# One written order of pieces for the set-up and the first two batches of a packed-attention and gated-MLP kernel, with its conversion adds on one engine

## Chip, core and metric

The kernel runs on one core of a Trainium2 chip. The engines that matter are TensorE (PE in the profile, with its weight loads as PEld), VectorE (DVE), ScalarE (ACT), GpSimd (POOL) and SyncE (SP), whose queue issues every data transfer. The metric is the device time of one execution in microseconds, median of several runs, lower is better.

## What is computed

Eight batches, 576 positions, 8 heads of 64 channels, 512 model channels. Attention goes through 32 packed queries per head; a gated product with a five-tap convolution and a second MLP with a mix over positions follow. Shortened from the reference:

```python
def sm_attn(qq, kk, vv):
    s = scale * np.matmul(qq, kk.transpose(0, 1, 3, 2))
    a = np.exp(s - np.max(s, axis=-1, keepdims=True))
    a = a / (np.sum(a, axis=-1, keepdims=True) + 1e-09)
    return np.matmul(a, vv)
p_packed = sm_attn(p, k, v)              # 32 packed rows per head
x = sm_attn(q, p_packed, p_packed)       # back to 576 positions
...
gate = 1.0 / (1.0 + np.exp(-gate_pre))   # gate_pre: conv_w over 5 taps of x
x = gate * (x @ w_val) @ w_out
...
h = np.maximum(x @ w_in, 0.0)
u, v = h[..., :512], h[..., 512:]
v_n = (v - mu) / np.sqrt(var + 1e-06)    # normalised over channels
v_s = np.einsum('ts,bsd->btd', w_spatial, v_n) + b_spatial[None, :, None]
out = (u * v_s) @ w_out2
```

## The kernel before

**Set-up.** The weight matrices arrive as 64-bit floats. Each of four matrices (`w_outT`, the two halves of `w_in`, `w_val`) is loaded in four pieces of 128 rows, 128x1024 words or 512 KB each (`load_raw`, L484), and each piece is converted to 32 bits by `from_f64` (L456): one ACT instruction (L460), then three on DVE (L464, L467, L468), then an add (L471). The add runs on POOL, or on DVE for the five pieces that `DADD` names: two of `w_outT` (`o0`, `o1`), two of the second half of `w_in` (`w0`, `w1`) and one of its first half (`u2`). The four converted pieces are called `woT`, `winv` (second half of `w_in`), `wval` and `winu` (first half). Pieces of `winu` share one temporary buffer (`cv_p`, one buffer), so the next piece's ACT instruction waits for the add of the piece before. `fold` (L499) multiplies `woT` with `winv` or `winu` on PE into the split weight `wp`, which takes the place of both matrices from then on: four folds for the `v` half (`fv`), four for the `u` half (`fu`). `spatial` (L509) loads and splits the position mix into `ws`; for its last rows it loads 128 rows (L517) and then 97 rows (L520). `final` (L527) does the same as `from_f64` for `w_out2`.

**Attention of a batch** (`Attn`): `sa` (packed scores and softmax, L141 to L163), `tr` (transposes, L172), `av` (L181), `ppt` (L204), `sb` (scores back, L212, and two softmaxes in `softmax_n`, L224 to L230), `sb2` (L236 to L243, with the split `Ah`/`Al`), `m` (packed rows times `wval`, L256, split into `Mh`/`Ml`), then the gate: for the first batch by `cx` on PE (L291, with the sigmoid at L299), for the others by `xt` and a convolution on DVE (L310).

**MLP of a batch** (`Mlp`): `val` (products of the `M` and `A` splits, 48 matmuls in four groups, one for each 128 channels, then gate and split), `hv` (five row blocks, normalised over channels into `vn`), `hu` (four groups), `sp` (four groups of the mix over positions), `out` (four groups). All PE results go through one pool of four accumulators (`ps2`).

**Order.** Three lists of tokens, `START` (set-up and the first batch's attention), `FIRST` (first batch's MLP, the second's attention) and `LOOP` (each later batch's MLP and the next batch's attention), give the order in which the pieces are written; each token writes out a whole piece. The kernel is built with a scheduler that places the instructions of all engines from there. Matmuls of 32-bit inputs appear twice in the counts of the trace.

Of the kernel before, what the change touches and what calls it, by code (L numbers as in the profile page):

```python
# [31 lines left out]
def packed_attention_gated_mlp(  # L32
# [72 lines left out]
    def load_kq(kind, b, g):  # L105
        src = kT if kind == "k" else qT
        t = kq_p.tile([P, 2, S], F32, tag="kq", name="kq")
        nc.sync.dma_start(out=t, in_=src[b, g])
        kq_t[kind, b, g] = t

    def load_v(b, g):
        t = v_p.tile([P, 4, 5, 65], F32, tag="v", name="v")
        nc.sync.dma_start(out=t, in_=vT[b, g])
        v_t[b, g] = t

    def load_p(b):
        t = sm_p.tile([P, NC * NPK], F32, tag="pbd", name="pbd")
        nc.sync.dma_start(out=t, in_=pT[b])
        pbd_t[b] = t

    class Attn:
        def __init__(self, b):
# [3 lines left out]
            self.gate = {}  # L126

# [8 lines left out]
        def sa(self, _):  # L136
            ps, heads = self.heads(pbd_t.pop(self.b), "k")
            for i in range(0, 8, 2):
                for qt in range(4):
                    for g, h, pT_, k in heads[i:i + 2]:  # L140
# [4 lines left out]
                        )  # L145
            mx = sm_p.tile([P, 8], F32, tag="mx", name="mx")
# [13 lines left out]
            for g in range(2):  # L160
                a = f_p.tile([P, S], F32, tag="f", name="a")
# [8 lines left out]
        def tr(self, g):  # L170
            aT = sm_p.tile([P, NB, NPK], F32, tag="aT", name="aT")
            nc.vector.transpose(out=aT.rearrange("p a b -> p (a b)"), in_=self.a.pop(g))  # L172
            self.aT[g] = aT

        def av(self, g):
# [12 lines left out]
            if g == 0:  # L188
# [3 lines left out]
            nc.vector.reciprocal(rs, rs)  # L192
            nc.scalar.activation(out=self.pp[:, g, :], in_=ps[:, :64], func=AF.Copy, scale=rs)
            if self.b == 0:
                if g == 0:
# [6 lines left out]
        def ppt(self, _):  # L202
            ps = ps2.tile([P, 2, 512], F32, tag="ps2", name="ps2")[:, 0, :P]
            nc.tensor.transpose(ps, self.pp.rearrange("p a b -> p (a b)"), ident)  # L204
            self.ppT = pp_p.tile([P, P], F32, tag="ppT", name="ppT")
            nc.scalar.copy(out=self.ppT, in_=ps)

        def sb(self, _):
# [8 lines left out]
            for g in range(2):  # L217
                self.softmax_n(g, ps[g])

        def softmax_n(self, g, ps):  # L220
# [8 lines left out]
            )  # L229
            nc.scalar.activation(out=sTf, in_=sTf, func=AF.Exp, scale=scale)  # L230
            self.sT[g] = sT

        def sb2(self, g):
# [9 lines left out]
            nc.vector.transpose(out=an, in_=sT.rearrange("p a b -> p (a b)"))  # L243
            hi = am_p.tile([P, S], F32R, tag="Ah", name="Ah")
            lo = am_p.tile([P, S], F32R, tag="Al", name="Al")
            split(hi, lo, an)
            self.A[g] = (hi, lo)
            self.an[g] = an

        def m(self, _):  # L250
            ps = ps2.tile([P, 2, 512], F32, tag="ps2", name="ps2")
            for h in range(4):
                hs = slice(NPK * h, NPK * h + NPK)
                for g in range(2):
# [4 lines left out]
                    )  # L259
            hi = am_p.tile([P, 2, DM], F32R, tag="Mh", name="Mh", bufs=1)  # L260
            lo = am_p.tile([P, 2, DM], F32R, tag="Ml", name="Ml", bufs=1)
            split(hi, lo, ps)
            self.M = (hi, lo)

        def xt(self, n):
# [9 lines left out]
            if n == 0:  # L275
# [3 lines left out]
            if n == 1:  # L279
                for c in range(4):  # L280
                    self.conv(c, self.x[c // 2][:, c % 2, :])

        def cx(self, n):
            ps = [ps2.tile([P, 2, 512], F32, tag="ps2", name="ps2") for _ in range(2)]
            for tap in reversed(range(CONV)):
                sft = CONV - 1 - tap
                lo = sft if n == 0 else 0
                for h in range(4):
                    hs = slice(NPK * h, NPK * h + NPK)
                    for g in range(2):  # L290
# [12 lines left out]
        def conv(self, c, x):  # L303
            gt = ug_p.tile([P, S], F32, tag="ug", name="gate")
            self.gate[c] = gt
            acc = f_p.tile([P, S], F32, tag="f", name="acc")
            nc.scalar.activation(out=acc, in_=x, func=AF.Copy, scale=cw[:, c, CONV - 1:CONV])  # L307
            for tap in range(CONV - 1):
# [4 lines left out]
                )  # L313
            nc.scalar.activation(out=gt, in_=acc, func=AF.Sigmoid)

    class Mlp:
        def __init__(self, at):
# [3 lines left out]
            self.vn = None  # L321

        def val(self, c):
# [3 lines left out]
            for n in range(2):  # L327
# [7 lines left out]
                )  # L335
            t = f_p.tile([P, S], F32, tag="f", name="g1")
            nc.vector.tensor_tensor(  # L337
                out=halves(t), in0=ps[:, :, :SH], in1=halves(at.gate.pop(c)), op=ALU.mult
            )
            g = g_p.tile([P, 2, S], F32R, tag="g", name="g")  # L340
            split(g[:, 0, :], g[:, 1, :], t)
            if not self.g1:
# [4 lines left out]
            self.g1[c] = g  # L347

        def hv(self, tt):
# [11 lines left out]
            vr = vr_p.tile([P, DM], F32, tag="vr", name="vr")  # L361
            if w == P:
                mm3(ps, [((g1[k][:, 0, ts_], g1[k][:, 1, ts_]), (w_hi[k], w_lo[k])) for k in range(NC)])
                nc.scalar.activation(out=vr, in_=ps, func=AF.Relu)  # L364
            else:
                mms(ps, [(self.tail[:, k, :], wk) for k in range(NC) for wk in (w_hi[k], w_lo[k])])
                nc.scalar.copy(out=vr[:w], in_=ps[w:])
                nc.vector.tensor_tensor(out=vr[:w], in0=ps[:w], in1=vr[:w], op=ALU.add)
                nc.scalar.activation(out=vr[:w], in_=vr[:w], func=AF.Relu)
            st = sm_p.tile([P, 6], F32, tag="st", name="st")  # L370
# [4 lines left out]
            nc.vector.tensor_scalar_add(rstd[:w], mv[:w, 1:2], 1e-6)  # L375
            nc.gpsimd.tensor_tensor(out=rstd[:w], in0=rstd[:w], in1=mhalf[:w], op=ALU.pow)  # L376
            nc.vector.tensor_scalar(  # L377
                out=vr[:w], in0=vr[:w], scalar1=mv[:w, 0:1], scalar2=rstd[:w],
                op0=ALU.subtract, op1=ALU.mult,
            )  # L380
            if tt < NT - 1:
                split(vn[0][:, tt, :], vn[1][:, tt, :], vr)
            else:
                split(vn[0][:64, tt, :], vn[0][64:, tt, :], vr[:w])
                nc.scalar.copy(out=vn[1][:64, tt, :], in_=vr[:w])

        def hu(self, c):
            ps = ps2.tile([P, 2, 512], F32, tag="ps2", name="ps2")
            cs = slice(P * c, P * c + P)
            for n in range(2):  # L390
# [10 lines left out]
                )  # L401
            u = ug_p.tile([P, S], F32, tag="ug", name="u")
            nc.scalar.activation(out=halves(u), in_=ps[:, :, :SH], func=AF.Relu)
            self.u[c] = u

        def sp(self, c):
            ps = ps2.tile([P, 2, 512], F32, tag="ps2", name="ps2")
            cs = slice(P * c, P * c + P)
            for n in range(2):
# [12 lines left out]
                )  # L422
            t = f_p.tile([P, S], F32, tag="f", name="g2")
            nc.vector.tensor_tensor(  # L424
                out=halves(t), in0=ps[:, :, :SH], in1=halves(self.u.pop(c)), op=ALU.mult
            )
            g = g_p.tile([P, 2, S], F32R, tag="g", name="g")
            split(g[:, 0, :], g[:, 1, :], t)
            self.g2[c] = g

        def out(self, e):
            ps = ps2.tile([P, 2, 512], F32, tag="ps2", name="ps2")
            cs = slice(P * e, P * e + P)
            for n in range(2):
# [10 lines left out]
                )  # L445
            t = f_p.tile([P, S], F32, tag="f", name="o")
            nc.scalar.copy(out=halves(t), in_=ps[:, :, :SH])  # L447
            nc.sync.dma_start(out=outT[self.b, e], in_=t)
# [7 lines left out]
    def from_f64(dst, raw, n, pool, tag, last=nc.gpsimd):  # L456
# [5 lines left out]
        )  # L462
        ci, ei = c.bitcast(I32), e.bitcast(I32)
# [6 lines left out]
        )  # L470
        last.tensor_tensor(out=dst, in0=dst, in1=c, op=ALU.add)  # L471

    def raw64(slot, srcs):
        n = len(srcs)
        raw = (vn_p if slot == "vn1" else const).tile([P, n, 512, 2], I32, tag=slot, name="raw")
        for i, src in enumerate(srcs):
# [197 lines left out]
```

## Time and profile before

| | us |
|---|---|
| median of 3 runs | 637.4 (636.73 to 638.5) |
| the profiled execution, its own time | 639.22 |
| its span in the trace | 637.4 |

The profile is of one execution; its time is 1.82 us above its span, and the median of the runs lies 1.8 us below the profiled execution's own time. Times in the trace count from the span's start. "Busy" is the time in which an engine has an instruction; "idle before" is the time in which it had none, with the event that ended it. The granted clock is 1.00 at full speed (2.4 GHz) and 0.50 at half (1.2 GHz).

### The profile page before, as it was taken

The page shows a single profiled execution, that of the slowest core. Times are in us where ns is not written, and L with a number is a line of the kernel's source. Part 1 is how long each engine was busy: PE and PEld are TensorE (multiplying, and loading weights), DVE is VectorE, ACT ScalarE, POOL GpSimd, SP SyncE. Part 2 cuts the span into 40 slices and gives each one's busy share as a digit, 9 for nine tenths or more (in the row PEclk, how much of TensorE's full clock was granted, in tenths as well). Part 3 has the DMA queues.
Part 4 walks back from the last instruction along what each step waited for, and adds up shares of the span by engine and source line. Part 5 has one row for each costly group of instructions (what it writes and reads, how often), then busy time and mean ns, then how long its engine had stood idle before and what let it go on. Part 6 is the DMA issues. An engine that isn't in the chain of part 4 may idle for free.

```text
span 637.4 us, 12474 instructions
## 1 busy us (share of the span) xinstructions
PE 596.7 (94%) x5267; PEld 514.7 (81%) x5267; DVE 446.0 (70%) x873; ACT 292.3 (46%) x503; POOL 49.3 (8%) x67
## 2 busy tenths in 40 slices
PE   3687697999999999999999999999999999999997
PEld 2323663898988898899889888989889988989997
DVE  4998355977957696687759685869667875965640
ACT  2522435636463564346543655355533744363422
POOL 1242002200010000100010001000010001000100
PEclk9985797999999999999999999999999999999999
DMA  8960053302322012401222132202240110010001
GB/s 331 408 226 1 1 194 124 127 1 76 114 88 76 20 59 77 159 1 76 80 85 75 53 102 86 75 20 77 64 149 1 75 39 1 2 57 20 1 1 74
DMA packets 16569, 52.48 MB, mean 82 GB/s; under 512 B 1953, under 2 KB 2977, under 8 KB 16514
## 3 DMA queue, kind: packets, MB, share of 16 engines
q1 hardware_dynamic: 16514, 51.70, 22.7%
q8 instruction: 41, 0.67, 0.4%
q14 instruction: 14, 0.11, 0.1%
HBM read 42.25 MB, written 9.44 MB: 81 GB/s over the span
## 4 chain that ended last, share of the span: by engine, by line
PE 80%; DVE 9%; DMA 5%; ACT 3%; POOL 1%; issue 1%; SPq 0%; ACTq 0%; POOLq 0%
PE ps L95 72%; DMA raw<-w_outT 3%; DMA stage<-wsT 2%; PE ps L141 2%; DVE mx L148 2%; PE ps L271 1%; PE ps L181 1%; PE ps L212 1%; ACT L163 1%; DVE tmp L467 1%; PE ps L256 1%; ACT a L163 1%; DVE tmp L464 1%; DVE m L154 1%; POOL winu L471 1%
## 5 line engine op out<-in xcount | busy, mean ns | idle before, releaser
L95 PE MATMUL ps<-ws,vn 128*128 128x288 f32 (+1 forms) x896 | 124.0, 296 | 0.0
L95 PEld LDWEIGHTS ps<-ws,vn 128*128 128x128 f32 (+1 forms) x896 | 120.3, 188 | 2.9 <-issue 2.8
L95 PE MATMUL ps<-g,wp 128*128 128x288 f32 x768 | 113.6, 297 | 0.0
L95 PEld LDWEIGHTS ps<-g,wp 128*128 128x128 f32 x768 | 106.8, 188 | 4.4 <-DVE g L337 1.3
L95 PEld LDWEIGHTS ps<-g,wo 128*128 128x128 f32 x768 | 102.2, 188 | 6.1 <-issue 3.5
L95 PE MATMUL ps<-g,wo 128*128 128x288 f32 x768 | 105.6, 296 | 0.0
L95 PE MATMUL ps<-wp,g 128*128 128x512 f32 x384 | 98.7, 402 | 3.2 <-ACT a L163 3.2
L310 DVE SCALAR_TENSOR_TENSOR acc<-x,cw,acc 128x572 f32<-128x572 f32 (+3 forms) x112 | 82.6, 813 | 24.7 <-ACT acc L307 24.7
L95 PEld LDWEIGHTS ps<-wp,g 128*128 128x128 f32 x384 | 69.6, 188 | 22.1 <-ACT a L163 5.2
L90 ACT CAST g<-g 128x576 fp32r<-128x576 f32 x64 | 43.2, 674 | 73.7 <-DVE g L424 57.1
L376 POOL TENSOR_TENSOR rstd<-rstd,mhalf 128x1 f32<-128x1 f32 (+1 forms) x40 | 24.2, 606 | 460.7 <-DVE rstd L375 460.7
L91 DVE TENSOR_TENSOR g<-g,g 128x576 fp32r<-128x576 f32 x64 | 49.3, 772 | 11.0 <-ACT g L90 10.3
L371 DVE BATCH_NORM_STATS2 st<-vr 128x6 f32<-128x512 f32 (+1 forms) x40 | 27.5, 690 | 30.0 <-ACT vr L364 26.9
L95 PE MATMUL ps<-Ah,Mh 128*128 128x288 f32 x128 | 39.1, 305 | 5.1 <-ACT gate L299 5.1
L90 ACT CAST vn<-vr 128x512 fp32r<-128x512 f32 (+1 forms) x40 | 24.7, 618 | 33.5 <-DVE vr L377 33.5
L95 PE MATMUL ps<-Ah,Ml 128*128 128x288 f32 x128 | 39.0, 305 | 0.0
L95 PE MATMUL ps<-Al,Mh 128*128 128x288 f32 x128 | 39.0, 304 | 0.0
L424 DVE TENSOR_TENSOR g<-ps,u 128x576 f32<-128x576 f32 x32 | 24.1, 754 | 19.1 <-PE ps L95 19.0
L377 DVE TENSOR_SCALAR vr<-vr,mv,rstd 128x512 f32<-128x512 f32 (+1 forms) x40 | 21.5, 538 | 22.5 <-POOL rstd L376 22.4
L447 ACT COPY o<-ps 128x576 f32<-128x576 f32 x32 | 20.3, 635 | 34.8 <-PE ps L95 34.8
L91 DVE TENSOR_TENSOR vn<-vr,vn 128x512 fp32r<-128x512 f32 (+1 forms) x40 | 27.1, 680 | 11.4 <-ACT vn L90 11.3
L364 ACT ACTIVATE vr<-ps 128x512 f32<-128x512 f32 x32 | 19.5, 611 | 30.2 <-PE ps L95 17.4
(111 smaller groups left out, 735.8 us busy)
## 6 DMA issues: line engine op xcount, KB each, us to landing
v<-vT SPq DMA_DIRECT2D x16, 650.0 KB, 5.1
kq<-kT SPq DMA_DIRECT2D x16, 576.0 KB, 4.3
kq<-qT SPq DMA_DIRECT2D x16, 576.0 KB, 4.8
outT<-o SPq DMA_DIRECT2D x32, 288.0 KB, 2.1
raw<-w_in SPq DMA_DIRECT2D x8, 512.0 KB, 10.6
raw<-w_outT SPq DMA_DIRECT2D x4, 512.0 KB, 8.7
raw<-w_val SPq DMA_DIRECT2D x4, 512.0 KB, 9.4
raw<-w_out SPq DMA_DIRECT2D x4, 512.0 KB, 5.2
```

Of the source, the lines that this page charges most:

```text
L90: nc.scalar.copy(out=hi, in_=src)
L91: nc.vector.tensor_tensor(out=lo, in0=src, in1=f32(hi), op=ALU.subtract)
L95: nc.tensor.matmul(out, lhsT=a, rhs=b, start=(i == 0), stop=(i == len(pairs) - 1))
L141: nc.tensor.matmul(ps[g][NPK * qt:NPK * qt + NPK, h // 2, SQ * (h % 2):SQ * (h % 2) + SQ], lhsT=pT_, rhs=k[:, SQ * qt:SQ * qt + SQ], start ...
L148: nc.vector.tensor_reduce(mx[:, 4 * g:4 * g + 4].rearrange("p (a b) -> p a b", a=2), ps[g][:, :, :SH].rearrange("p a (b c) -> p a b c", b= ...
L310: nc.vector.scalar_tensor_tensor(out=acc[:, sft:], in0=x[:, :S - sft], scalar=cw[:, c, tap:tap + 1], in1=acc[:, sft:], op0=ALU.mult, op1=A ...
L364: nc.scalar.activation(out=vr, in_=ps, func=AF.Relu)
L371: nc.vector.bn_stats(st[:w], vr[:w])
L376: nc.gpsimd.tensor_tensor(out=rstd[:w], in0=rstd[:w], in1=mhalf[:w], op=ALU.pow)
L377: nc.vector.tensor_scalar(out=vr[:w], in0=vr[:w], scalar1=mv[:w, 0:1], scalar2=rstd[:w], op0=ALU.subtract, op1=ALU.mult,)
L424: nc.vector.tensor_tensor(out=halves(t), in0=ps[:, :, :SH], in1=halves(self.u.pop(c)), op=ALU.mult)
L447: nc.scalar.copy(out=halves(t), in_=ps[:, :, :SH])
```

## The change

The three lists become two. `HEAD` orders the set-up, the first two batches' MLPs and the attention of batches one to three. Pieces are now generators that stop at each `yield`; a token such as `0hv1.1` runs one part of a piece (batch 0, `hv`, block 1), a token without a number after the point runs the rest. All of `HEAD` stands inside `tc.manual_schedule()`, so that the engines' instructions stand in the order that is written; `LOOP` serves batches three to eight and goes through the scheduler as before. `DADD` is empty: all adds of the conversion are POOL's. The second load of the last spatial rows takes all 128 rows in place of 97. The softmaxes of `sb` and the convolutions of `xt` become pieces of their own (`sn`, `cv`).

```diff
-DADD = ('u2', 'o0', 'o1', 'w1', 'w0')
-START = """
-ik0 ip0 ro0 ic0 ik1 sa0 iv1 uo0 iv0 rw0 tr0 lv0 rv0 ro1 uo1 cw0 rv1 cb0 lk0 lq0 rw1 uw0 tr1 uo3 uw1 av0 uw2 uo2 uv0 av1 uv1 uw3 lq1 fv3 fv0 fv1 lk1 ppt0 sb0 sb20 sb21 fv2 uv3 uv2 lp0 m0 cx0 cx1 lv1
...
+DADD = ()
+HEAD = """
+ro1.1 cb0.1 ip0 ro0 ic0 ik0 rw1 rw0.1 uo2.1 ik1 uo2.1 lk0 uo0.1 lp0 uo2 uo0.1 uo1.1 ro1 cw0.1 iv1 uo1.1 uo0 iv0 cw0.1
...
     def split(hi, lo, src):
         nc.scalar.copy(out=hi, in_=src)
+        yield
         nc.vector.tensor_tensor(out=lo, in0=src, in1=f32(hi), op=ALU.subtract)
...
         nc.scalar.activation(
             out=c, in_=raw.bitcast(F32)[:, :, 1], func=AF.Prelu, scale=2.0 ** -112, alpha=2.0 ** 32
         )
+        yield
+        dst = dst()
...
+        yield
         last.tensor_tensor(out=dst, in0=dst, in1=c, op=ALU.add)
...
-        st = f_p.tile([P, S], F32, tag="f", name="stage")
-        nc.sync.dma_start(out=st[:97], in_=wsT[:97, t + 1, :])
+        nc.sync.dma_start(out=st, in_=wsT[:, t + 1, :])
+        yield
...
+    def run(order, batch):
+        live = {}
         for tok in order.split():
...
+            tok, _, n = tok.partition(".")
+            name = tok.lstrip("01")
+            b = batch if len(name) == len(tok) else int(tok[0])
+            if tok not in live:
+                live[tok] = steps(b, name[:-1], int(name[-1]))
+            for _ in itertools.islice(live[tok], int(n) if n else None):
+                pass
...
-    run(START, -1, at, None)
-    for b in range(B):
-        ml = Mlp(at)
-        at = Attn(b + 1) if b + 1 < B else None
-        run(FIRST if b == 0 else LOOP, b, at, ml)
+    with tc.manual_schedule():
+        run(HEAD, -1)
+    for b in range(2, B):
+        run(LOOP, b)
```

What this does to the engines' own orders is shown at three places. The first is ACT ahead of the first batch's gate. `tmp<-raw` is the conversion's ACT instruction, `wp` a fold's result, `Mh` and `Ah` the splits of `m` and `sb2`, `gate` the sigmoid of `cx`. Before:

```order
L506 CAST wp_101<-ps_432 128x512
L460 ACTIVATE tmp<-raw 128x512
L230 ACTIVATE sT<-sT 128x576
L90 CAST Mh<-ps_453 128x1024
L90 CAST Ah<-an 128x576
L460 ACTIVATE tmp<-raw 128x512
L90 CAST Ah<-an 128x576
L460 ACTIVATE tmp<-raw 128x512 x3
L299 ACT_TABLE_LOAD
L299 ACTIVATE gate<-ps_466 128x288 x2
L299 ACTIVATE gate<-ps_467 128x288 x2
```

And ACT now:

```order
L566 CAST wp_101<-ps_428 128x512
L519 ACTIVATE tmp<-raw 128x512 x2
L114 CAST Ah<-an 128x576
L566 CAST wp_101<-ps_446 128x512
L339 ACT_TABLE_LOAD
L339 ACTIVATE gate<-ps_462 128x288 x2
L339 ACTIVATE gate<-ps_463 128x288 x2
L339 ACTIVATE gate<-ps_510 128x288 x2
L339 ACTIVATE gate<-ps_511 128x288 x2
L519 ACTIVATE tmp<-raw 128x512
L114 CAST Mh<-ps_568 128x1024
L566 CAST wp_101<-ps_582 128x512
```

The gate's sigmoids stood behind the last three conversions of `winu`; now they stand ahead of the last three, and `Mh` stands behind one conversion of `winu` (the second piece). The two conversions in the second row are the last two pieces of `wval`.

The second place is DVE ahead of the first `val`. The three instructions of a conversion end in `wval<-raw` or `winu<-raw`. Before, from `Ml` on:

```order
L91 TENSOR_TENSOR Ml<-ps_453,Mh 128x1024
L237 TENSOR_SCALAR sm_421<-sm_421 128x18
L91 TENSOR_TENSOR Al<-an,Ah 128x576
L471 TENSOR_TENSOR winu<-winu,tmp 128x512
L238 RECIPROCAL sm_421<-sm_421 128x18
L239 TENSOR_TENSOR sT<-sT,sm_421 128x576
L464 TENSOR_SCALAR tmp<-tmp 128x512
L243 STREAM_TRANSPOSE an<-sT 128x576
```

And DVE now, from the last conversion of `wval` to `Ml` (with the buffers' numbers):

```order
L525 TENSOR_SCALAR tmp_453<-tmp_453 128x512
L528 TENSOR_SCALAR tmp_453<-tmp_453 128x512
L529 SCALAR_TENSOR_TENSOR wval_100<-raw_390,tmp_453 128x512
L525 TENSOR_SCALAR tmp_402<-tmp_402 128x512
L528 TENSOR_SCALAR tmp_402<-tmp_402 128x512
L529 SCALAR_TENSOR_TENSOR winu_563<-raw_282,tmp_402 128x512
L525 TENSOR_SCALAR tmp_584<-tmp_584 128x512
L528 TENSOR_SCALAR tmp_584<-tmp_584 128x512
L529 SCALAR_TENSOR_TENSOR winu_563<-raw_282,tmp_584 128x512
L116 TENSOR_TENSOR Ml_588<-ps2_568,Mh_587 128x1024
L568 TENSOR_TENSOR wp1_102<-ps2_582,wp0_101 128x512
```

The second half of the second softmax, whose end (`an`) `cx` needs, stood behind `Ml`. Now both halves stand ahead of the last two conversions of `wval`; between the first of those and the row shown first stand the two splits `Al` and two folds' results. `Ml` stands behind two conversions of `winu`.

The third place is SP's queue of loads, around `w_val` (`raw` is a weight piece, `kq` keys or queries, `stage` spatial rows). Ahead of the rows shown stood two `kq`, a `pbd`, the first two pieces of `w_outT`, the 20 KB of `conv_w`, two `v` and two pieces of `w_in`. Before:

```order
L477 DMA raw<-w_outT 128x1024 x2
L108 DMA kq<-kT 128x1152
L108 DMA kq<-qT 128x1152
L477 DMA raw<-w_in 128x1024 x2
L118 DMA pbd<-pT 128x128
L477 DMA raw<-w_val 128x1024 x2
L108 DMA kq<-qT 128x1152
L118 DMA pbd<-pT 128x128
L113 DMA v<-vT 128x1300 x2
L477 DMA raw<-w_val 128x1024 x2
L477 DMA raw<-w_in 128x1024 x4
```

And SP now, from the first two pieces of `w_val` to the last two; ahead of the rows shown stand three `kq`, two `pbd`, all four pieces of `w_outT`, three pieces of `w_in`, `conv_w` and two `v`:

```order
L545 DMA raw<-w_val 128x1024 x2
L545 DMA raw<-w_in 128x1024
L133 DMA kq<-qT 128x1152 x2
L572 DMA stage<-wsT 128x576 x3
L545 DMA raw<-w_in 128x1024 x2
L139 DMA v<-vT 128x1300
L572 DMA stage<-wsT 128x576
L139 DMA v<-vT 128x1300
L145 DMA pbd<-pT 128x128
L545 DMA raw<-w_in 128x1024
L545 DMA raw<-w_val 128x1024 x2
```

Four spatial loads and three pieces of the first half of `w_in` stood behind the last two pieces of `w_val` and now stand ahead of them. On PE the set of instructions is the same; the `sa` of the third batch now stands ahead of the first batch's `sp`, and each `m` stands right behind its batch's `sb`.

## Rows read from the trace of the kernel before

**Rows 1.** The page, first part: busy time, share of the span and instructions by engine

```profile
PE 596.7 (94%) x5267; PEld 514.7 (81%) x5267; DVE 446.0 (70%) x873; ACT 292.3 (46%) x503; POOL 49.3 (8%) x67
```

**Rows 2.** Stretches: start and end, length, busy by engine, granted clock, DMA share, GB/s

```profile
70.26:118.12 47.86, 43.03 (x314) 29.49 (x314) 28.24 (x65) 21.94 (x45) 5.30 (x6) 0.87 0.31 106
70.26:76.26 6.00, 6.00 (x25) 6.00 (x26) 1.52 (x2) 2.44 (x7) 0.00 (x0) 0.50 0.00 0
102.02:107.02 5.00, 5.00 (x45) 2.76 (x46) 3.89 (x9) 2.21 (x4) 1.78 (x2) 0.50 0.36 93
118.12:230.03 111.91, 111.38 (x992) 102.33 (x986) 84.64 (x156) 56.42 (x92) 7.86 (x9) 1.00 0.22 77
161.36:600.00 438.64, 435.42 (x3966) 391.44 (x3965) 321.07 (x634) 216.25 (x369) 18.10 (x33) 1.00 0.18 62
600.00:637.40 37.40, 33.38 (x244) 32.65 (x242) 10.40 (x18) 8.01 (x13) 1.10 (x2) 0.98 0.09 32
```

**Rows 3.** PE in order of time: start, length, work, count, idle before

```profile
49.43 1.93 PE L256 MATMUL ps<-wval,ppT 64*32 64x512 f32 x8 [3.07 <-POOL wval L471]
...
70.26 0.61 PE L95 MATMUL ps<-Ah,Mh 128*128 128x288 f32 x1 [5.05 <-ACT gate L299]
...
145.98 1.09 PE L256 MATMUL ps<-wval,ppT 64*32 64x512 f32 x16
```

**Rows 4.** ACT in order of time

```profile
26.39 0.68 ACT L460 ACTIVATE tmp<-raw 128x512 f32<-128x512 f32 x1 [0.17 <-DMA raw<-w_val]
27.69 0.67 ACT L460 ACTIVATE tmp<-raw 128x512 f32<-128x512 f32 x1 [0.62 <-DMA raw<-w_val]
...
63.95 0.68 ACT L460 ACTIVATE tmp<-raw 128x512 f32<-128x512 f32 x1 [2.90 <-POOL winu L471]
67.53 0.66 ACT L460 ACTIVATE tmp<-raw 128x512 f32<-128x512 f32 x1 [2.89 <-POOL winu L471]
68.20 1.28 ACT L299 ACT_TABLE_LOAD   x1
```

**Rows 5.** DVE in order of time

```profile
16.30 0.43 DVE L464 TENSOR_SCALAR tmp<-tmp 128x512 int32<-128x512 int32 x1 [0.77 <-ACT tmp L460]
16.76 0.43 DVE L467 TENSOR_SCALAR tmp<-tmp 128x512 int32<-128x512 int32 x1
...
17.70 0.77 DVE L172 STREAM_TRANSPOSE aT<-a 128x576 f32<-128x576 f32 x1
18.40 0.65 DVE L471 TENSOR_TENSOR winv<-winv,tmp 128x512 f32<-128x512 f32 x1
...
27.40 1.38 DVE L467 TENSOR_SCALAR tmp<-tmp 128x512 int32<-128x512 int32 x1
...
36.52 0.85 DVE L224 STREAM_TRANSPOSE sT<-ps 128x288 f32<-128x288 f32 x2
...
53.11 1.21 DVE L91 TENSOR_TENSOR Ml<-ps,Mh 128x1024 fp32r<-128x1024 f32 x1
```

**Rows 6.** POOL in order of time

```profile
27.10 1.39 POOL L471 TENSOR_TENSOR winv<-winv,tmp 128x512 f32<-128x512 f32 x1 [4.00 <-DVE winv L468]
...
36.48 1.26 POOL L471 TENSOR_TENSOR winv<-winv,tmp 128x512 f32<-128x512 f32 x1 [0.97 <-DVE winv L468]
```

**Rows 7.** Stretches again, for what the DMA engines moved (last two columns)

```profile
0.00:8.00 8.00, 1.21 (x32) 0.74 (x32) 0.94 (x4) 1.94 (x2) 2.08 (x8) 1.00 0.73 246
8.00:27.67 19.67, 12.47 (x136) 7.60 (x136) 17.21 (x44) 8.29 (x21) 2.55 (x3) 1.00 1.03 411
89.00:97.00 8.00, 8.00 (x30) 5.27 (x28) 2.61 (x5) 0.82 (x2) 1.28 (x1) 1.00 0.37 121
```

**Rows 8.** The chain that ended last, 80 to 104 us, its longest piece

```profile
83.95 13.35 DMA stage<-wsT
```

**Rows 9.** PE's waits over the whole run: us in total, times, longest

```profile
PE ps L181 <- DVE wp L507: 4.2, 1, 4.2
```

**Rows 10.** The page, groups of instructions: busy, mean ns | idle before

```profile
L424 DVE TENSOR_TENSOR g<-ps,u 128x576 f32<-128x576 f32 x32 | 24.1, 754 | 19.1 <-PE ps L95 19.0
```

More of the change, by code (lines that the diff above doesn't have):

```diff
@@ L1 @@
+import itertools
 from contextlib import ExitStack
@@ L216, in sb, with sn @@
                     )
-            for g in range(2):
-                self.softmax_n(g, ps[g])
-        def softmax_n(self, g, ps):
+            self.sps = ps
+            yield
+        def sn(self, g):
+            ps = self.sps[g]
             sT = f_p.tile([P, NB, NPK], F32, tag="f", name="sT")
@@ L278, in xt @@
                 nc.scalar.copy(out=self.x[j][:, :, ss], in_=ps[j][:, :, :SH])
-            if n == 1:
-                for c in range(4):
-                    self.conv(c, self.x[c // 2][:, c % 2, :])
+            yield
         def cx(self, n):
@@ L295, in cx @@
                         )
+            yield
             for c in range(4):
-                if n == 0:
+                if c not in self.gate:
                     self.gate[c] = ug_p.tile([P, S], F32, tag="ug", name="gate")
@@ L339, in val @@
             )
+            yield
             g = g_p.tile([P, 2, S], F32R, tag="g", name="g")
-            split(g[:, 0, :], g[:, 1, :], t)
-            if not self.g1:
+            self.g1[c] = g
+            yield from split(g[:, 0, :], g[:, 1, :], t)
+            if self.tail is None:
                 self.tail = vr_p.tile([P, NC, P], F32R, tag="tail", name="tail", bufs=1)
@@ L422, in sp @@
                 )
+                yield
             t = f_p.tile([P, S], F32, tag="f", name="g2")
@@ L426, in sp @@
             )
+            yield
             g = g_p.tile([P, 2, S], F32R, tag="g", name="g")
-            split(g[:, 0, :], g[:, 1, :], t)
             self.g2[c] = g
+            yield from split(g[:, 0, :], g[:, 1, :], t)
         def out(self, e):
@@ L470, in from_f64 @@
         )
+        yield
         last.tensor_tensor(out=dst, in0=dst, in1=c, op=ALU.add)
[L473 to L476, printed above, removed]
-            nc.sync.dma_start(out=raw[:, i], in_=words(src))
-        return [raw[:, i] for i in range(n)]
     woT, winv, winu = [], [], []
@@ L597, in packed_attention_gated_mlp, with load_cw @@
-    at = Attn(0)
+    def load_cw():
+        nc.sync.dma_start(out=cw64, in_=words(conv_w))
+        yield
+    ats = [Attn(b) for b in range(B)]
+    mls = [Mlp(at) for at in ats]
+    setup = {
+        "cw": lambda i: from_f64(lambda: cw.rearrange("p a b -> p (a b)"), cw64, NC * CONV, *early),
+        "cb": lambda i: tap_rows(),
+        "ro": lambda i: load_raw(f"o{i}", ("wo20", "ws1")[i], w_outT, 0),
+        "rw": lambda i: load_raw(f"w{i}", ("wo21", "vn1")[i], w_in, DM),
+        "rv": lambda i: load_raw(f"v{i}", ("wo20", "wo21")[i], w_val, 0),
+        "ru": lambda i: load_raw(f"u{i}", ("ws1", "wo20")[i], w_in, 0),
+        "uo": lambda k: unit("o", k, lambda: woT[k], early),
+        "uw": lambda k: unit("w", k, lambda: winv[k], early),
+        "uv": lambda k: unit("v", k, lambda: wval[:, k, :], early),
+        "uu": lambda k: unit("u", k, lambda: u_half(k), late),
+        "fv": lambda m: fold(m, 1),
+        "fu": lambda m: fold(m, 0),
+        "ws": spatial,
+        "wo": final,
+        "ip": load_p,
+        "ik": lambda i: load_kq("k", 0, i),
+        "iv": lambda i: load_v(0, i),
+        "ic": lambda i: load_cw(),
+    }
```

196 lines of the change are left out of this document (122 added, 74 removed).

## Prediction

> **What bounds the kernel now.** I read the page's busy times first, then the stretches, then PE in order of time. PE is busy 596.7 of 637.4 us [rows 1], so all of PE's idle time is 40.7 us. The stretches tell where it is [rows 2]: 3.2 us in the 438.6 us from 161.36 to 600, and 4.0 us in the last 37.4. What is left, 33.5 us, lies ahead of 161.36, in the set-up and the first batch. There PE is idle and it is also slow: the granted clock is 0.50 from 70.26 to 76.26, right behind a wait of 5.05 us, and again from 102.02 to 107.02, behind one of 4.2 us [rows 2, 3, 9]. From the second batch's `val` (161.36) on, the kernel is a PE-bound loop with nothing to win. So the question is how early the loop can start.
>
> I use three landmarks: the first `val` product (70.26, [rows 3]), the first `hu` product (118.12) and the third batch's `val` (230.03), whose stretches stand in [rows 2]. Between the first and the last of them PE does the same work in both kernels, in another order; from the third on the instruction order is that of before, and I carry its 407.4 us over unchanged.
>
> **Ahead of the first `val`.** Now the last thing that `val` waits for is the gate: ACT converts the pieces of `winu` ahead of it, 3.58 us apart (63.95 to 67.53), because each waits about 2.9 us for POOL's add of the piece before (one temporary buffer), and only then loads the sigmoid's table at 68.20 [rows 4]. In the changed order the gate stands ahead of those three. That removes this wait; what is late next is the last of `wval`, then `m`, then its split `Ml`.
>
> When do the last pieces of `w_val` land? The DMA engines moved 246 GB/s in the first 8 us (1.97 MB) and 411 GB/s from there [rows 7], so 10.05 MB by 27.67. The second piece of `w_val` stood at 9.08 MB in the old queue (adding up the sizes of the loads ahead of it) and ACT began on it at 27.69, having waited for it [rows 4]: a load lands when some 1 MB more than its own place has been moved. In the new queue the fourth piece stands at 14.87 MB: 15 weight pieces of 0.524, five `kq` of 0.590, four `v` of 0.666, four spatial loads of 0.295, and 0.22 of small ones. It lands at 8 + (15.84 − 1.97) / 0.411 = 41.7 us; the third at 40.5.
>
> From there the chain is counted on DVE. A conversion takes it 1.40 us (16.30 to 17.70), and a two-input split about 0.6 to 0.7 (18.40's add is 0.65) [rows 5]. POOL's add takes 1.39 us, and a conversion that follows at once is held by it: the second instruction takes 1.38 us instead of 0.43 (27.40, beside POOL's 27.10) [rows 5, 6], 0.95 us more. With ACT's 0.67 and a fold's result ahead of it in its queue, the third piece of `wval` reaches DVE at about 42.7. Then: conversion 1.4, held 0.95, two splits and two folds' results 2.6, conversion of the fourth piece 1.4, to 49.0; the first `winu` piece, held and converted, 2.35, to 51.4; POOL's add 1.4 and ACT 0.67, since this is still the one-buffer chain, and the second `winu` piece 1.4, to 54.9; `Ml` 1.14 (1.21 less its overlap, [rows 5]), to 56.0. `Mh` is ready before. `val` needs `Ml` in its third matmul, 0.65 us behind its first, so the first may start at 55.4. `cx` is not in this chain: both softmaxes end near 42 by the same counting, and it lies under the rest. **This term is 70.26 − 55.4 = 14.9 us earlier.** Its bounds: without any holding by POOL (three times 0.95) and with half the extra 1 MB (1.2 us), 19 us; with `m` and the last `v`-half fold at the half clock (3.8 for `m` at the pace of 49.43, where eight of 16 took 1.93, against 1.09 at full clock, [rows 3], and about 3 more for the fold), 9 us.
>
> **The five adds.** DVE loses five adds at 0.6 us each, 3.0 us. But by the row at 27.40 each add on POOL can cost DVE 0.95 us, if DVE's next instruction is of the kind that is held. The transposes at 36.52 were not, beside POOL's add of 36.48 [rows 5, 6]. So the move is worth between −1.8 and +3.0 us of DVE time; I take nothing, and the holdings on the chain are already counted above. The Trainium skill, "SBUF — State Buffer", section "Who interferes with whom", says that a GpSimd instruction that reads SBUF and a VectorE instruction with two SBUF inputs, or in a two-port mode, exclude each other for a whole instruction. By that rule alone, with every add in the way, all five would cost 4.8 us on DVE and save 3.0, and the first term would be 1.8 us smaller; the rows show the holding and, at 36.52, also its exception.
>
> **From the first `val` to the first `hu`.** Before, 47.86 us, with PE busy 43.03 [rows 2]. At full clock the two half-clock stretches, 11.0 us, would take 5.5, so the work is 37.5 us. To it comes the second batch's `m`, which is done here now: 1.1 us (145.98, [rows 3]). The 4.2 us wait [rows 9] goes: its chain begins in a load of 97 spatial rows that took 13.35 us [rows 8], through whose last 8 us the DMA share is only 0.37 [rows 7] with other loads in it; the load is now whole, like the other spatial loads, and no longer stands ahead of `av` on ACT and DVE. One new wait: `fu` needs the fourth `winu` piece, two more rounds of the one-buffer chain (7.1 us behind 54.9, and POOL's add, 63.5), and PE reaches it at about 55.4 + 6.4 + 1.2 = 63.0; I take 1 us. **47.9 − 39.6 = 8.3 us earlier.** Bounds: 9.3 without the wait, 2.5 if PE starts `val` at the half clock again (3.0) and one wait like the 2.9 of [rows 4] is left.
>
> **From the first `hu` to the third `val`.** Before, 111.9 us with 0.5 idle [rows 2]. Now `m` is gone from it (1.1 us), and the order is fixed: each engine takes what is written next, ready or not. I see three places for a wait: `sp` needs the last spatial split, which stands last on DVE ahead of it (by my count DVE has about 35 us of work left when `val` has ended and PE about 32 until `sp`'s first use); the second `val` needs the last convolution; and the second batch's first `hv` needs the last split of `val`, without pieces of `hu` and `sa` laid between as the loop has them. Between nothing and 3.5 us each; I take 4 in all. **2.4 us later.** Bounds: 1.6 earlier to 9 later.
>
> **Sum.** 14.9 + 8.3 − 2.4 = 20.8 us. The profiled execution took 639.22 us, 1.82 above its span; the changed kernel in the same conditions takes 618.4, and against the median of 637.4, which is 1.8 lower, **616.6, rounded to 617 us**. The bounds add up to 30 and to 2.5 us.
>
> **Rivals.**
> *A, the chain ahead of `val` is longer than counted.* ACT serves its queue in order, and `Mh` stands behind a `winu` conversion that waits for POOL; if the last `w_val` pieces land 5 us later or `winu`'s chain is held once more, `val` starts at 61 to 64. For it: SP issues the last two `w_val` pieces into a buffer that holds a `winv` piece until DVE has converted it, near 32 us. Against: the queue is full until then. 624 to 630 us.
> *B, the fixed order fits everywhere.* No holding on the chain, no new waits: 607 to 610 us. Against: three fixed places where I count no slack.
> *C, slower: the four accumulators.* In a fixed order a product that waits for a free accumulator holds all that follows on PE. One half of the second batch's `sb` is read by DVE only behind the last spatial split, so three of four accumulators serve `hu`, and two of `hu`'s four results are read by ACT behind a split of `w_out2` that waits for POOL. Reading a result takes 0.75 us (DVE, [rows 10]). If each of the 32 products of the first two batches (`val`, `hu`, `sp`, `out`, four each) waited that long, 24 us would be lost: 641 us. It decides from about 0.65 us a product. Against: the loop runs with the same four at 0.5 us idle in 68 us of each batch.
> *D, no change.* The gain ahead of `val` is given back at the three places, 637: it takes all bounds on the bad side at once, and a little more.
>
> Forecast (610 to 624) 0.60, A 0.19, B 0.10, D 0.05, C 0.06. A measurement of this kernel can tell about 0.3% (1.9 us) from no change: faster by more than that 0.89, within it 0.05, slower 0.06. The range that leaves out the far part of A and B, C and D is **607 to 629 us**.
>
> **What would show it.** Right: the sigmoid's table load comes before 51 us; the first `val` starts between 53 and 59; PE waits no more than 2 us ahead of `fu` and not at all for an `av`; the last spatial load lands within 5 us of its issue; `hu` starts near 95 and the third `val` near 209; from there on 407 us. Wrong: the last `wval` conversion on ACT after 46 us (A); a clock of 0.50 behind `val`'s start for more than 6 us; in the first two batches waits of PE for ACT's or DVE's reads that add up to over 9 us (C).

## The result and the profile after

The changed kernel took 616.45 us (615.56 to 617.28, four runs) against 637.95 us for the kernel before beside it: a ratio of 0.966, interval 0.9638 to 0.9688. The forecast was 617 us in 607 to 629. The profiled execution took 615.56 us, its span is 613.6 us. The busy times of the page answer to [rows 1]:

```profile
PE 581.7 (95%) x5267; PEld 507.2 (83%) x5267; DVE 451.1 (74%) x868; ACT 291.9 (48%) x503; POOL 54.7 (9%) x72
```

PE has the same 5267 matmuls and is busy 15.0 us less; its idle time fell from 40.7 to 31.9 us. Ahead of the first `val` it is busy 32.56 us at a granted clock of 1.00, where it was busy 41.66 at a mean of 0.87. The stretches show it (to the first `val`, from there to the first `hu`, to the third `val`, to the end, and the 6 us behind the first `val`; columns as in [rows 2]):

```profile
0.00:54.62 54.62, 32.56 (x396) 16.50 (x397) 44.41 (x88) 23.18 (x46) 19.98 (x22) 1.00 0.80 309
54.62:96.38 41.76, 39.15 (x331) 25.84 (x330) 37.12 (x79) 23.06 (x44) 13.28 (x14) 1.00 0.33 104
96.38:206.36 109.98, 109.33 (x969) 101.99 (x970) 89.66 (x154) 55.93 (x94) 4.96 (x6) 1.00 0.20 69
206.36:613.60 407.24, 400.67 (x3575) 362.87 (x3573) 279.92 (x550) 189.76 (x322) 16.51 (x30) 1.00 0.16 58
54.62:60.62 6.00, 5.30 (x37) 4.83 (x36) 4.87 (x8) 2.61 (x4) 2.57 (x2) 1.00 0.01 1
```

The granted clock is 1.00 in all of them. The 6 us behind the first `val`, which ran at 0.50 before [rows 2], do so no longer: PE's row has no gap from 43.91 to 55.4 ahead of them, where before PE had waited 5.05 us. PE in order of time around the landmarks, as [rows 3]:

```profile
43.91 5.72 PE L330 MATMUL ps<-an,ppk 32*64 32x288 f32 x160
49.56 2.00 PE L295 MATMUL ps<-wval,ppT 64*32 64x512 f32 x16
51.49 3.70 PE L563 MATMUL ps<-winv,woT 128*128 128x512 f32 x8
54.62 0.69 PE L120 MATMUL ps<-Ah,Mh 128*128 128x288 f32 x1
55.15 0.29 PE L120 MATMUL ps<-Al,Mh 128*128 128x288 f32 x1
56.15 0.40 PE L120 MATMUL ps<-Ah,Ml 128*128 128x288 f32 x1 [0.70 <-DVE Ml L116]
...
96.38 13.06 PE L120 MATMUL ps<-g,wp 128*128 128x288 f32 x96 [0.80 <-DVE wp L568]
```

`cx` (L330), `m` (L295), the last `v`-half fold (L563) and `val` follow one another, and the only wait in PE's row is the third `val` product's for `Ml`. Another is hidden inside `m`, which takes 2.00 us where the second batch's takes 1.06 (at 94.52): its last weight loads waited for POOL's add of the last `wval` piece (49.06 below). The weight loads have a row of their own:

```profile
50.51 0.14 PEld L295 LDWEIGHTS ps<-wval,ppT 64*32 64x32 f32 x4 [0.78 <-POOL wval L533]
```

ACT in order of time, as [rows 4]:

```profile
41.42 0.69 ACT L519 ACTIVATE tmp<-raw 128x512 f32<-128x512 f32 x1
42.67 0.67 ACT L519 ACTIVATE tmp<-raw 128x512 f32<-128x512 f32 x1 [0.57 <-DMA raw<-w_val]
...
44.89 1.28 ACT L339 ACT_TABLE_LOAD   x1
46.62 1.32 ACT L339 ACTIVATE gate<-ps 128x288 f32<-128x288 f32 x4 [0.45 <-PE ps L330]
49.28 1.32 ACT L339 ACTIVATE gate<-ps 128x288 f32<-128x288 f32 x4 [1.34 <-PE ps L330]
52.77 0.67 ACT L519 ACTIVATE tmp<-raw 128x512 f32<-128x512 f32 x1 [2.18 <-POOL winu L533]
53.34 1.00 ACT L114 CAST Mh<-ps 128x1024 fp32r<-128x1024 f32 x1
```

The sigmoid's table is loaded at 44.89 (before: 68.20), and the gate waits for PE alone. DVE in order of time, from the third piece of `wval` to `Ml`, as [rows 5]:

```profile
43.61 0.38 DVE L525 TENSOR_SCALAR tmp<-tmp 128x512 int32<-128x512 int32 x1
...
44.97 0.75 DVE L116 TENSOR_TENSOR Al<-an,Ah 128x576 fp32r<-128x576 f32 x1
45.64 1.28 DVE L568 TENSOR_TENSOR wp<-ps,wp 128x512 fp32r<-128x512 f32 x2
...
47.50 0.42 DVE L525 TENSOR_SCALAR tmp<-tmp 128x512 int32<-128x512 int32 x1
...
48.90 0.42 DVE L525 TENSOR_SCALAR tmp<-tmp 128x512 int32<-128x512 int32 x1
49.35 1.39 DVE L528 TENSOR_SCALAR tmp<-tmp 128x512 int32<-128x512 int32 x1
...
53.47 0.43 DVE L525 TENSOR_SCALAR tmp<-tmp 128x512 int32<-128x512 int32 x1 [2.13 <-ACT tmp L519]
...
54.87 1.22 DVE L116 TENSOR_TENSOR Ml<-ps,Mh 128x1024 fp32r<-128x1024 f32 x1
```

And POOL's adds beside these, as [rows 6]:

```profile
45.13 1.73 POOL L533 TENSOR_TENSOR wval<-wval,tmp 128x512 f32<-128x512 f32 x1 [10.91 <-DVE wval L529]
49.06 1.39 POOL L533 TENSOR_TENSOR wval<-wval,tmp 128x512 f32<-128x512 f32 x1 [2.19 <-DVE wval L529]
51.47 1.27 POOL L533 TENSOR_TENSOR winu<-winu,tmp 128x512 f32<-128x512 f32 x1 [1.02 <-DVE winu L529]
55.03 1.27 POOL L533 TENSOR_TENSOR winu<-winu,tmp 128x512 f32<-128x512 f32 x1 [2.30 <-DVE winu L529]
```

One conversion is held (49.35, 1.39 in place of 0.43). The add of 45.13 holds nobody: it takes 1.73 itself.

`cx`, from whose results the gate is made, needs the end of the second softmax (`an`), and that moved too. DVE and PE before:

```profile
56.89 0.77 DVE L243 STREAM_TRANSPOSE an<-sT 128x576 f32<-128x576 f32 x1
57.71 7.49 PE L291 MATMUL ps<-an,ppk 32*64 32x288 f32 x152 [2.12 <-DVE an L243]
```

And DVE now:

```profile
42.90 0.78 DVE L281 STREAM_TRANSPOSE an<-sT 128x576 f32<-128x576 f32 x1
```

So `cx` ended at 65.20 before and ends at 49.63 now, 15.6 us earlier, which is as much as the first `val` gained.

PE's waits by what they waited for, over the whole run, the longest five (the four others are of 0.8 us and less):

```profile
PE ps L619 <- POOL cw L533: 13.9, 1, 13.9
PE ps L213 <- DVE aT L204: 5.6, 1, 5.6
PE ps L120 <- ACT a L194: 2.7, 5, 0.6
PE ps L239 <- ACT pp L227: 2.4, 2, 1.3
PE ps L120 <- DVE Ml L116: 1.1, 2, 0.7
```

The 4.2 us wait of `av` [rows 9] and the gate's 5.05 us are gone. In the DMA issues from 80 to 110 us the last spatial load, whole now, takes 3.0 us (before: 13.35 us, [rows 8]):

```profile
stage<-wsT SPq DMA_DIRECT2D x1, 288.0 KB, 3.0
```

### The profile page after: what moved, and what is told of

It is laid out like the page before. It is cut to its first block, busy times and chain, and to the rows that moved or that the text cites. A ratio compares the mean times of both kernels' runs of the same rounds, so it can differ in the third digit from the quotient of the medians.

```text
span 613.6 us, 12468 instructions
## 1 busy us (share of the span) xinstructions
PE 581.7 (95%) x5267; PEld 507.2 (83%) x5267; DVE 451.1 (74%) x868; ACT 291.9 (48%) x503; POOL 54.7 (9%) x72
## 4 chain that ended last, share of the span: by engine, by line
PE 74%; DVE 7%; ACT 3%; issue 1%; ACTq 0%
PE ps L120 68%; DVE acc L350 2%; PE ps L170 2%; PE ps L311 1%; DVE mx L178 1%; PE ps L213 1%; ACT L194 1%; PE ps L248 1%; PE ps L295 1%; ACT a L194 1%; DVE g L116 1%; ACT g L114 1%; DVE nb L189 1%; DVE m L184 1%; DVE g L480 0%
## 5 line engine op out<-in xcount | busy, mean ns | idle before, releaser
L350 DVE SCALAR_TENSOR_TENSOR acc<-x,cw,acc 128x572 f32<-128x572 f32 (+3 forms) x112 | 84.7, 815 | 20.5 <-ACT acc L346 19.7
L421 DVE BATCH_NORM_STATS2 st<-vr 128x6 f32<-128x512 f32 (+1 forms) x40 | 27.5, 689 | 26.3 <-ACT vr L409 23.7
```

Source lines behind the costliest of these rows:

```text
L350: nc.vector.scalar_tensor_tensor(out=acc[:, sft:], in0=x[:, :S - sft], scalar=cw[:, c, tap:tap + 1], in1=acc[:, sft:], op0=ALU.mult, op1=A ...
L421: nc.vector.bn_stats(st[:w], vr[:w])
```

## The experiments

Twelve runs were made, in four groups; each group has its own runs of the kernel before (medians 639.33, 639.45, 638.77 and 638.81 us), and ratios are to those. The changed kernel stood in one of these groups only, that of experiments 8, 11 and 12. Where another time is set against its 616.45 us, the two are from different groups, between which the kernel before differs by up to 1.5 us (637.95 to 639.45).

**1. The whole load alone, in the kernel before.**

```diff
-        nc.sync.dma_start(out=st[:97], in_=wsT[:97, t + 1, :])
+        nc.sync.dma_start(out=st, in_=wsT[:, t + 1, :])
```

> The kernel before, with one edit: the last spatial rows are loaded as 128 rows in place of 97. Order theory (the gain is mostly the earlier first val): the load no longer takes 13 us, so the 4.2 us wait ahead of av and the half clock behind it (2.5 us) go, and the first val stays near 70: 630 to 634 us. Rival, the load is most of the gain: 625 or less. Rival, the load was hidden anyway: 636 to 638.

632.9 us, ratio 0.990 [0.9879, 0.9923]. As expected: `av`'s wait is gone, the first `val` stays at 70.34, the first `hu` comes at 110.09 in place of 118.12.

**2. All adds on POOL alone, in the kernel before** (`DADD` empty).

> The kernel before, with one edit: all adds of the conversion on POOL. Order theory: an add on POOL holds DVE about as long as it saves, so within 2 us of before, 635.5 to 639.5. Rival, DVE bounds the set-up and the five adds are 3 us of it or more: 634 or less.

636.15 us, ratio 0.995 [0.9929, 0.9965]. The time lies in the range written for it, but that was worked from 637.4 us; beside its own runs of before it is 3.2 us faster, more than the nothing of the theory and as much as the 3 us of the rival, whose 634 it did not reach. The first `val` came at 68.84, 1.4 us earlier, and `hu` at 114.97. In the old order the move is worth something; the two experiments that follow find nothing in the new one.

**3. The five adds back on DVE, in the changed kernel.**

```diff
-DADD = ()
+DADD = ('u2', 'o0', 'o1', 'w1', 'w0')
```

> The changed kernel, with the five adds on DVE again. Order theory: four of them lie in the first 20 us, which loads and the first attention set, and the fifth falls ahead of fu: 615 to 618, no difference beyond 0.3%. Rival, the five adds are part of the gain: 619 or more.

616.47 us, 0.964 [0.9627, 0.9657]: no difference from the changed kernel's 616.45 us.

**4. All sixteen set-up adds on DVE.**

> The changed kernel, with all 16 adds of the set-up's conversions on DVE (those of w_out2 stay on POOL). Each costs DVE 0.6 us; on POOL it costs 0.95 where the next instruction is held, nothing where it is not. In DVE's stretch from 19 to 51 us there are six adds, of which the trace shows about three held: plus 3.6 minus 2.8, near 1 us later, and the one-buffer chain of winu gets 0.7 us a round shorter: 614.5 to 618. If POOL's adds were free: 620 or more. If all were held: 614 or less.

616.41 us, 0.964 [0.9626, 0.9655]. The conversion at 50.33 is not held now, but the adds stand in DVE's own queue:

```profile
50.33 0.43 DVE L528 TENSOR_SCALAR tmp<-tmp 128x512 int32<-128x512 int32 x1
...
51.28 0.69 DVE L533 TENSOR_TENSOR wval<-wval,tmp 128x512 f32<-128x512 f32 x1
51.88 0.69 DVE L533 TENSOR_TENSOR winu<-winu,tmp 128x512 f32<-128x512 f32 x1
...
54.70 1.22 DVE L116 TENSOR_TENSOR Ml<-ps,Mh 128x1024 fp32r<-128x1024 f32 x1
```

`Ml` begins at 54.70, against 54.87 with all adds on POOL. But the last `wval` piece is complete at 51.97 in place of 50.45, and the first `val` starts at 56.13 in place of 54.62; at the first `hu` (96.79, against 96.38) most of that is made up. So the time does not depend on where the adds stand. That POOL takes from DVE exactly what it saves it is not shown.

**5. 97 rows again, in the changed kernel** (the first diff, reversed).

> The changed kernel, with the last spatial rows loaded as 97 rows again. Order theory: the load is issued at 95 and takes 3.0 us whole; with 97 rows it takes about 13, ACT stands behind it from 98 to about 108 with the results of hu in its queue, and sp starts about 10 us later: 623 to 629. Rival, hidden under the 13 us of hu: 615.5 to 618.

623.8 us, 0.976 [0.9737, 0.9777]: 7.3 us above the changed kernel. The chain that ended last, ACT behind it, and PE's two new waits in order of time:

```profile
95.27 11.19 DMA stage<-wsT
```

```profile
106.48 0.67 ACT L585 CAST ws<-stage 32x576 fp32r<-32x576 f32 x1 [8.40 <-DMA stage<-wsT]
```

```profile
109.02 6.42 PE L120 MATMUL ps<-g,wp 128*128 128x288 f32 x36 [4.22 <-ACT u L459]
...
118.59 1.59 PE L120 MATMUL ps<-ws,vn 128*128 128x288 f32 x10 [1.19 <-DVE ws L116]
```

The load is nearly as slow in its new place, and what stands behind it in the fixed order waits: ACT's reads of `hu`'s results (`u`, L459) stand behind its conversion `ws`, so PE runs out of accumulators inside `hu`. From 109.0 to 112.0, behind that wait, the granted clock is 0.50. `sp` begins at 117.00 in place of 110.54.

**6. The gate behind `winu`'s conversions again, in the changed kernel.** `uu` are `winu`'s pieces; parts of `val` that stood between them are left out:

```diff
-uv3.1 cx0 0uu0.1 uv3 m0.1 cx1 0uu0 fv2.1 0uu1.1 fv2.1 m0.1 0uu1.1 fv2.2 m0 0uu1 ... 0uu2 ... 0uu3
+uv3.1 0uu0.1 uv3 0uu0 0uu1 0uu2 0uu3 cx0 m0.1 cx1 fv2.1 fv2.1 m0.1 fv2.2 m0 ...
```

> The changed kernel, with the three later conversions of winu put ahead of the gate again (and so ahead of m's split). Order theory: these conversions are 3.6 us apart on one buffer, the gate comes at about 63 in place of 50 and the first val at 64 to 67; some 2 us of it come back because fu no longer waits for winu: 622 to 628. Rival, DVE is busy all along and the gate's place makes no difference: 615.5 to 618.

628.85 us, 0.984 [0.9815, 0.9857]: 12.4 us above the changed kernel and just above what was expected, with the first `val` at 71.38, later than expected. ACT in order of time, and PE:

```profile
58.22 0.66 ACT L518 ACTIVATE tmp<-raw 128x512 f32<-128x512 f32 x1 [2.89 <-POOL winu L532]
61.77 0.66 ACT L518 ACTIVATE tmp<-raw 128x512 f32<-128x512 f32 x1 [2.89 <-POOL winu L532]
62.44 1.28 ACT L338 ACT_TABLE_LOAD   x1
```

```profile
64.50 1.96 PE L294 MATMUL ps<-wval,ppT 64*32 64x512 f32 x16 [12.60 <-ACT gate L338]
66.39 5.55 PE L562 MATMUL ps<-winv,woT 128*128 128x512 f32 x8
```

The expectation had the late gate delay `val` alone. In the new order of PE the first batch's `m` stands behind `cx` (and not right behind its `sb`), so a late gate delays `m` too: by the name of the wait, `cx`'s four results fill the four accumulators until the sigmoids have read them, so `m`, the fold behind it and `Mh` all stand behind the gate, and PE sits idle for 12.6 us. It comes back at a granted clock of 0.50 (64.5 to 66.5).

**7. The same lists through the scheduler,** without the fixed order.

```diff
-    with tc.manual_schedule():
-        run(HEAD, -1)
+    run(HEAD, -1)
```

> The changed kernel without manual_schedule: the same written order, but the scheduler may place the instructions of the first two batches. Order theory: what counts is where pieces stand, and the scheduler keeps most of it: 615 to 621, first val at 53 to 60. Rival, the fixed order itself is the gain: 628 or more.

639.64 us, 1.001 [0.9991, 1.0022]: the whole gain is gone. The theory was wrong here and the rival right. The run holds the whole load too, worth 6.4 us in the old order (experiment 1), so through the scheduler the new lists lose about what that load gives. The first `val` comes at 78.83 and the first `hu` at 122.09; from there to the end it takes 515.4 us, against 517.2 with the fixed order. ACT and PE ahead of `val`:

```profile
58.92 0.68 ACT L519 ACTIVATE tmp<-raw 128x512 f32<-128x512 f32 x1 [5.25 <-POOL winu L533]
...
69.60 0.66 ACT L519 ACTIVATE tmp<-raw 128x512 f32<-128x512 f32 x1 [2.90 <-POOL winu L533]
70.28 1.28 ACT L339 ACT_TABLE_LOAD   x1
```

```profile
72.34 1.96 PE L295 MATMUL ps<-wval,ppT 64*32 64x512 f32 x16 [12.54 <-ACT gate L339]
```

The scheduler put the gate behind all of `winu`'s conversions once more, although the list has it ahead of the last three of them.

**8. The same with a second temporary buffer for `winu`** (pieces 0 and 2).

```diff
-        "uu": lambda k: unit("u", k, lambda: u_half(k), late),
+        "uu": lambda k: unit("u", k, lambda: u_half(k), late if k % 2 else early),
```

> The changed lists without the fixed order, as in the run before (639.64 us, first val at 78.83), and the winu pieces 0 and 2 take their temporary from the other pool, so that the conversions ahead of the gate no longer follow one another through one buffer. Theory (in the run before, val was late because each of winu's conversions on ACT waited 2.9 us for POOL's add of the piece before, and the scheduler had put the gate behind all four): two to three of these waits go, the table load comes at 62 to 65 instead of 70.3, val starts at 70 to 73, and the time is 631 to 635 us. Rival (the scheduler's order of loads, folds and softmaxes is late as a whole, and the waits for POOL only fill time in which the gate's own input was not there): val stays at 77 or later and the time is 637 to 642 us.

637.45 us, 0.997 [0.9947, 0.9986]. The time is the rival's, and the landmarks lie between the two: the table load comes at 66.33 and `val` at 75.36, 3.5 us earlier than in experiment 7, and the time falls by 2.2 us (2.6 by the ratios, as the groups differ). So what the second buffer gives back is a small part of that loss. The trace shows something else that is late: the last steps of the second softmax (`an`) begin at 50.7 and 52.7 us where the changed kernel has them at 39.5 and 42.9, and `cx` ends near 60 in place of 50. That the rest of the loss comes of this is not shown.

**9. Fixed only up to the first `hu`,** the rest of the same list through the scheduler.

```diff
+    first, rest = HEAD.split("CUT")
     with tc.manual_schedule():
-        run(HEAD, -1)
+        run(first, -1, live)
+    run(rest, -1, live)
```

> The changed lists, fixed as written only up to the first hu; from there on the rest of the same list goes through the scheduler. Theory (all of the gain lies ahead of the first hu, and the run without any fixing lost its 23 us there: first hu at 122.1 instead of 96.4, and 515.4 us from there to the end against 517.2): the first hu stays at 96 to 97.5 and the time is 613 to 619 us. Rival (the fixed order between the first hu and the third val is needed too, because the scheduler moves the softmaxes or the spatial splits there): 622 us or more, with hu at 96 to 97.5 but the third val at 214 or later.

616.62 us, 0.964 [0.9614, 0.9669]: the full gain, as the theory had it. In the profiled run the first `val` came at 56.34, the first `hu` later than expected (99.22, behind a wait of 2.0 us for `wp`), and the third `val` at 209.65; that execution took 617.96 us, the slowest of its five.

**10. `Mh` and `Ml` ahead of `winu`'s second conversion,** with the second buffer of experiment 8, fixed order throughout.

```diff
-0uu0 fv2.1 0uu1.1 fv2.1 m0.1 0uu1.1 fv2.2 m0 0uu1
+0uu0 fv2.1 m0.1 fv2.1 m0 0uu1.1 0uu1.1 fv2.2 0uu1
```

> The changed kernel with two edits meant to shorten the chain ahead of val: Mh and Ml ahead of the second winu conversion on ACT and DVE, and the first and third winu conversions in other temporary buffers, so that no conversion waits for an add before it. If the chain through Ml sets the first val, val's third product moves from 56.2 to about 54.6 (the fold ahead of it ends there), and DVE loses its 2.1 us wait: 614 to 615.5. If DVE's work as such is the bound up to hu, hu starts no earlier: 616 to 617.

615.15 us (614.61 to 615.62), 0.962 [0.9605, 0.9635]: 1.3 us below the changed kernel's 616.45, but from another group of runs.

**11 and 12. That version and the changed kernel, side by side.**

> The changed kernel as it is, once more beside the next one: 615.5 to 617.3 us, as measured before; first val near 54.6.

> The version with Mh and Ml ahead of winu's second conversion and with the second temporary buffer, once more, on the same chip as the changed kernel. Theory (the one-buffer chain still held the second winu conversion ahead of Ml, and winu's last piece held a fold): 614.5 to 615.7 us, 1 to 2 us below the changed kernel of the same call, hu about 1 us earlier. Rival (what is won ahead of hu is given back in the fixed order behind it; the 1.3 us of the first run were the chip's): within 0.5 us of the changed kernel.

615.7 us (0.9645 [0.9619, 0.9671]) for the changed kernel and 615.84 us (0.9642 [0.9618, 0.9667]) for the version: the rival was right, no difference. `Ml`'s wait of 0.7 us is gone from the version's trace, and no time with it. In the changed kernel's second profile the first `val` starts at 55.33 in place of 54.62: between two executions of one kernel this landmark moves by 0.7 us.

## Why the prediction was right, step by step

The sum was 20.8 us earlier; between the profiled executions it is 639.22 − 615.56 = 23.7 us, between the medians 637.95 − 616.45 = 21.5. That the forecast of 616.6 lies within 0.2 us of the median is in part luck: the three terms miss by 0.7, −2.2 and 4.3 us, and the profiled execution of the changed kernel is the fastest of its four.

**Ahead of the first `val`: 14.9 predicted, 15.6 measured** (70.26 to 54.62). That the gate must stand ahead of `winu`'s conversions is shown: with it behind them again `val` is back at 71.38 and 12.4 us are lost (experiment 6). How much of the 15.6 us is the gate's own is not. Before, PE waited 5.05 us for it behind `cx`; now `m` and a fold fill the 5.0 us between `cx` and `val`, and `cx` itself ends 15.6 us earlier, since the later half of the second softmax begins its last step at 42.90 in place of 56.89. The prediction's count has this in it, for it lets both softmaxes end near 42 (measured 43.68); but its reading of the old chain names the gate alone. No run moved the softmaxes by themselves.

The count on DVE was met in its steps: the first `winu` piece was to begin at 49.0 and began at 48.90, `Ml` was to end at 56.0 and PE took it at 56.15. This chain set only the third product, though: the first stood behind `m` and a fold on PE, and with `Ml`'s wait gone the time was the same (experiment 12). In the count two errors cancelled. The last `w_val` piece landed at 42.7 (ACT's wait at 42.67), not 41.7, and DVE began on the third at 43.61, not 42.7; and the first of the two holdings counted did not come, since behind that conversion stood `Al`, and POOL's add (45.13, 1.73 us) waited in its place.

At 44.97 DVE had begun on `Al` when POOL's add came (45.13), at 49.06 POOL came first, and each time the later one took longer. The Trainium skill, "SBUF — State Buffer", section "Who interferes with whom", says that: which of the two is issued first decides who blocks. It also says that a VectorE instruction with one SBUF input is not held outside the two-port modes; `Ml`, whose other input is an accumulator, took 1.22 us beside the add of 55.03, as it did before [rows 5], and the trace agrees. The transposes at 36.52, which the prediction calls an exception to the holding, read an accumulator and nothing in SBUF (`sT<-ps`, [rows 5]), so they are no exception to that.

What the prediction did not price is what a late gate costs in the new order of PE: `m` behind `cx`, 12.6 us of waiting (experiment 6).

**The five adds: nothing predicted, nothing measured** (experiments 3 and 4). By the rule of the Trainium skill ("SBUF — State Buffer", section "Who interferes with whom") alone, with every add in the way, the first term was estimated 1.8 us smaller with them on POOL; the time did not change either way. In the old order the move alone gave 0.5% (experiment 2). The cause of that stays open.

**First `val` to first `hu`: 8.3 predicted, 6.1 measured** (47.86 to 41.76). This term was too large. PE is busy 39.15 us where 38.6 were counted as work, and idle 2.61 where 1.0 was: 0.70 for `Ml`, 1.11 for `pp` and 0.80 for `wp`. The one wait that was foreseen, `fu`'s for the last `winu` piece, did not come: PE's 16 folds from 63.62 took 7.13 us, without a gap. In its place came three that were not foreseen, on results that stand in the queues of ACT and DVE; DVE is busy 37.12 of 41.76 us there. The whole load is worth what its wait and its half clock cost: 6.4 us in the old order (experiment 1), 7.3 us in the new one (experiment 5).

**First `hu` to third `val`: 2.4 later predicted, 1.9 earlier measured.** This is the step with the wrong sign. PE is busy 109.33 of 109.98 us: the three places at which the fixed order was to wait, priced at 4 us, cost 0.65 in all. Experiment 9 says the same from the other side: with this part left to the scheduler the time does not change. The three places were guesses at unknown waits, and their bound of nothing was the nearest. **From the third `val` on: 407.4 carried over, 407.24 measured.**

**The rivals.** A (ACT's last `wval` conversion after 46 us): it stood at 42.67. C (accumulators, 24 us): from the first `val` to the third PE is idle 2.61 + 0.65 = 3.3 us for all causes. The mechanism is real, but it strikes where a reader is late, in experiments 5 and 6. D did not happen. B's mechanism did, behind `hu`, where 0.65 us of waiting was all.

**What the prediction did not ask** is how much the new lists bring without the fixing. Through the scheduler they give nothing (experiment 7). What gains is the lists with the fixing, and the fixing only ahead of the first `hu` (experiment 9); the old lists in a fixed order were not run. Of experiment 7's loss of 23.2 us (639.64 − 616.45) the gate's place is worth 12.4 us by experiment 6, if the two are the same; the buffer chain alone is 2.2 us (experiment 8). The softmaxes that end 10 us later were seen there, but not moved by themselves, so their share stays open.

## What to carry to other kernels

Where a set-up chain runs over four engines, find the last thing that the first main product waits for, and ask what stands ahead of it on its own engine without being needed: here three conversions that each waited 2.0 to 2.9 us for another engine's add. Then see which accumulators or buffers the late reader holds, since the products behind it wait too. PE came back at a granted clock of 0.50 from the waits of 5.05 and 4.2 us before [rows 2], of 4.22 us in experiment 5 and of 12.6 us in experiment 6, so that such a wait cost more than its length. Writing the pieces in a better order is not enough where a scheduler places them: look at where the instructions ended up, and fix the order there; behind the first `hu`, fixing brought and cost nothing (experiment 9).

## What was not expected of the hardware

A transfer of 97 rows took 13.35 us [rows 8] and, in another place, 11.19 us (experiment 5), where 128 rows took 3.0 us: three quarters of the bytes, some four times as long. The Trainium skill, "DMA: Bandwidth & Descriptors", section "Why a DMA increments its semaphore by 16 and not by 1", says that a transfer is spread over the largest number of engines, up to 16, that divides its rows: 16 for 128 rows, and for 97, a prime, one. The durations agree in direction. So does the stretch from 102 to 106 us of experiment 5, in which the load was still under way; columns as in [rows 2]:

```profile
102.00:106.00 4.00, 2.79 (x21) 2.56 (x20) 0.00 (x0) 0.00 (x0) 0.00 (x0) 1.00 0.07 25
```

A mean share of 0.07 over 16 engines is about one of them at work, at 25 GB/s.

The granted clock does not tell all. Behind the wait of 5.6 us in the changed kernel's set-up it reads 1.00, yet each of the 80 matmuls of `av` (L213, from 24.79) takes about 315 ns there and 220 ns in the second batch (from 87.17). These runs do not say why.
